# The attention of the first two batches on 64-row tiles, with a new order for every engine

## The chip, the cores and the metric

The kernel runs on one core of one Trainium2 chip. Times are device microseconds (us) of one execution of the whole program; the number that counts is the median of several runs. A profile comes from one further execution, in which each instruction's start and length was recorded. Names: PE is the matrix engine (PEld its weight loads), DVE the vector engine, ACT the scalar engine, POOL the GpSimd engine and SP the queue that issues most of the DMAs.

## The reference, cut to what matters

```python
kv  = einsum('bhsd,bhse->bhde', k, v)          # 8 batches, 8 heads, 576 rows, 64 columns
out = einsum('bhsd,bhde->bhse', q, kv)
x   = out / sqrt(mean(out**2) + 1e-6) * g_norm # per row and head
x   = x.transpose(0, 2, 1, 3).reshape(8, 576, 512)
u, v = split(relu(x @ w_in), 2)                # w_in is 512 x 1024
v   = (v - mean(v)) / sqrt(var(v) + 1e-6)
out = (u * (w_spatial @ v + b_spatial)) @ w_out
```

The attention has no softmax: per head it is two small products, a 64 x 64 matrix from 576 rows of keys and values, and 576 rows of queries times that matrix. The weights `w_in` and `w_out` arrive as 64-bit floats and are decoded on the chip.

## The kernel before

The eight heads of a batch are taken as four pairs. 512 of the 576 rows are the main part, four chunks of 128; the last 64 rows of two batches are put side by side and form a tail tile. The attention of a pair is a step K (keys times values, evicted from PSUM to SBUF as a small matrix), a step A or D (queries times that matrix, then squares and their sums), a step B (reciprocal root, and the scaling of the rows), and a step T (a transpose, whose eviction applies `g_norm` and writes x transposed). Then come the products with `w_in` (v half: H and `hv`, u half: u and `u_unit`), the layer norm, the spatial product (s, `sp_0`, `sp_steps`) and the output product (`out_unit`).

Batches 2 to 7 already do their attention on tiles of 64 rows and 64 columns, four of which lie in the array at once (`part_k`, `part_q`, `part_t`, `square`, `normal`, `turn_over`, `tail_norm`, `tail_turn`, scheduled by `later_steps`); they work on two pairs at a time. Batches 0 and 1 use functions of their own: `att_k` (from L202, products at L209) makes a 128 x 128 block-diagonal matrix of two heads, and `att_qa` (product at L284) multiplies queries of 128 rows by it; `norm_a` and `norm_b` square and scale 512 columns, `att_t` transposes four 128 x 128 blocks, and `att_end`, `tail_a`, `tail_b` and `att_tail` do the tail rows.

Batch 0 is special in its products with `w_in`: while the weights are being loaded and decoded, x is kept as one fp32 tile (X32) and H, u and h run in fp32 (L625, L663, L631). All later products use pairs of fp32r tiles, high and low part, in three products (L571, L538, L804). One H is `psv[c] += X32[pair k, chunk c] * W32[k]`, so H of pair k needs T of pair k and the k-th decoded weight.

The opening (batch 0, the attention of batch 1, and the loading, decoding and splitting of all weights) is written out by hand as a list of steps, `PLAN`. Its letters: L lets the next attention load go, W issues the next weight load (`w_in` in eight pieces of 512 KB, W0 to W7; then `w_spatial`, `b_spatial`, `w_out`), c and C decode a weight piece (one ACT instruction, then five of DVE, L954 to L958), H, u, h, s are the products above, e, F, f, y the ReLU, layer norm and splitting of v, X and E the splitting of weights into high and low part, Y sums of weights, Q and O decoding and splitting of a piece of `w_out`. At the end of the program the table `ORDER` gives, for each engine, the order of all its instructions, as positions in what is left of the program's own order; each engine runs strictly in that order.

In the opening PSUM has four banks for the products (`ps_mm`), three single banks for the attention and one for the tail; after it the last four banks become two slots of two banks each.

Of the kernel before, what the change touches and what calls it, by code (L numbers as in the profile page):

```python
# [33 lines left out]
PINNED = (mybir.EngineType.PE, mybir.EngineType.Activation, mybir.EngineType.SP)  # L34
PLAN = """

[ L W N8 G J00 L c C D00 W n6 L W J01 c B00 C L D01 J02 T00 B01 W D02 H00 c H30 H20 J03 T01 B02 D03
T02 H10 W c W H31 B03 L C L C H21 c H22 C H11 W W H32 a0 c W H01 T03 C c H02 H23 H03 H12 ] H33 e2
H13 e3 b0 L e1 C K10 F1 L L e0 W t0 c u00 C f2 F0 y2 L y0 F3 u01 D10 y1 W K12 u02 X3 a1 Z u03 L y3
u10 b1 X2 B10 t1 W W E1 L E0 A11 u11 W Q0 z u12 h D12 u13 W B12 T10 s s | s X1 T12 X0 s B11 D13 X5  # L40
B13 T11 X7 s s s s Y1 Y0 X4 P T13 O0 Q1 X6 W | p O1 R
# [21 lines left out]
""",  # L63
    "Activation": """
# [11 lines left out]
""",  # L76
    "DVE": """
# [21 lines left out]
""",  # L99
    "SP": """  # L100
# [3 lines left out]
""",  # L104
    "Pool": """
0.6 2.2 4.2 0.8 2 1 0.3 1 0 1 0 2 1 0.3 1 0.6 1 0 1 0
# [9 lines left out]
def body(ctx: ExitStack, tc, qT, qtl, kvm, kvt, g2, w_in, wsT, bsp, w_out, out):  # L116
# [9 lines left out]
    opening = ExitStack()  # L126
    ps_att = opening.enter_context(tc.tile_pool(name="ps_att", bufs=3, space=bass.MemoryType.PSUM))
    ps_tail = opening.enter_context(tc.tile_pool(name="ps_tail", bufs=1, space=bass.MemoryType.PSUM))
# [50 lines left out]
    def att_load(b, p, kind):  # L179
        if kind in "feko":  # L180
# [4 lines left out]
            r = p % 2 * TAIL if b > 1 else 0  # L185
            nc.sync.dma_start(kt[r:r + TAIL], kvt[b, p])
            keys[b, p] = kv, kt, None
# [4 lines left out]
        if kind == "k":  # L192
            qs = load.tile([P, P], F32, name="qs", tag="qs")
            nc.sync.dma_start(qs, qT[b, p, :, S - P:S])
            keys[b, p] = kv, kt, qs
# [6 lines left out]
    def att_k(b, pairs, st, copy=nc.vector.tensor_copy):  # L202
# [9 lines left out]
        for p in reversed(pairs):  # L212
            kv, kt, qs = keys.pop((b, p))
            for c in range(NC + 1):
                of = kv[:, :, c] if c < NC else kt
                for h in (0, D):
                    if first is None:
                        first = product(p, of, h, c).ins
                    else:
                        with tc.high_priority(), tc.issue_after(first):  # L220
                            product(p, of, h, c)
# [751 lines left out]
    def make_out(k):  # L973
# [3 lines left out]
        if pin:  # L977
            pin()
# [346 lines left out]
```

## Time and profile before

| what | us |
|---|---|
| median of 3 runs | 496.46 (495.97 to 496.64) |
| the profiled execution, its own time | 497.11 |
| its span, first to last instruction | 495.3 |
| PE busy, share of the span | 479.4 (97%) |
| DVE busy | 415.8 (84%) |
| ACT busy | 286.5 (58%) |
| POOL busy | 21.1 (4%) |

The span is what the trace covers; the 1.8 us between it and the execution's own time lie around it. An engine's busy time is the union of its instructions' lengths; instructions of one engine overlap by a little, so on an engine that never waits the cost of an instruction is the distance from its start to the next start, which is shorter than its length. The granted PE clock is 0.996 of full speed over the whole span.

### The profile page before, as it was taken

The numbers are of one execution on the slowest core, as the hardware profiler recorded it, in microseconds if no ns is written. First come the engines' busy times: TensorE is split into PE (matmuls) and PEld (weight loads), VectorE is DVE, ScalarE is ACT, GpSimd is POOL, SyncE is SP. The second block draws the span as 40 slices with busy tenths as digits, with TensorE's granted clock in tenths as the row PEclk, the third lists the DMA queues.
The fourth block names the chain that finished last, engine by engine and source line by source line (L and its number), as shares of the span: only waits on it lengthen the run. The fifth ranks groups of instructions, "written<-read, shape, count | busy, mean of one in ns | idle before, by whom it ended". The sixth has DMA issues, their size and how long they took to land.

```text
span 495.3 us, 11993 instructions
## 1 busy us (share of the span) xinstructions
PE 479.4 (97%) x4560; PEld 417.4 (84%) x4560; DVE 415.8 (84%) x1248; ACT 286.5 (58%) x913; POOL 21.1 (4%) x46
## 2 busy tenths in 40 slices
PE   6899999999999999999989999999999999999996
PEld 6658698798888899889977889988998899888985
DVE  1899889899899889988769789898888899998870
ACT  3757964697535855466423784547454587438331
POOL 5000000000000001000000001000000001000000
PEclk9999999999999999999989999999999999999999
DMA  7998100576524508135644514415571252215313
GB/s 240 356 337 271 42 3 21 154 249 242 181 71 149 194 7 297 50 98 174 227 156 149 171 44 151 159 65 161 163 273 56 44 192 89 84 44 170 108 73 98
DMA packets 28079, 71.99 MB, mean 145 GB/s; under 512 B 3506, under 2 KB 8626, under 8 KB 26484
## 3 DMA queue, kind: packets, MB, share of 16 engines
q1 hardware_dynamic: 24564, 49.19, 29.6%
q0 software_dynamic: 3456, 22.02, 13.4%
q8 instruction: 36, 0.59, 0.5%
q14 instruction: 23, 0.19, 0.1%
HBM read 58.09 MB, written 13.11 MB: 144 GB/s over the span
## 4 chain that ended last, share of the span: by engine, by line
PE 66%; DVE 13%; ACT 10%; DMA 8%; issue 2%; SPq 1%; POOL 0%; ACTq 0%; DVEq 0%
PE pso L538 18%; PE psh L571 10%; PE psb L804 6%; PE psa L804 6%; PE psub L804 4%; PE psc L804 4%; PE psh L625 3%; PE psuc L804 3%; DMA stage<-w_in 3%; PE psua L804 2%; DMA WO<-spare_o 2%; DMA qs<-qtl 2%; PE pskv L366 2%; DVE VL L575 2%; PE psu L663 1%
## 5 line engine op out<-in xcount | busy, mean ns | idle before, releaser
L538 PE MATMUL pso<-WO,G 128*128 128x512 f32 x384 | 98.3, 397 | 1.9 <-DMA WO<-spare_o 1.9
L538 PEld LDWEIGHTS pso<-WO,G 128*128 128x128 f32 x384 | 69.6, 189 | 16.8 <-DVE r L253 2.1
L574 ACT CAST G<-g 128x288 fp32r<-128x288 f32 (+1 forms) x56 | 22.8, 408 | 38.0 <-DVE g L823 37.8
L571 PE MATMUL psh<-WVH,XL 128*128 128x512 f32 x112 | 43.7, 390 | 0.0
L571 PE MATMUL psh<-WVL,XH 128*128 128x512 f32 x112 | 43.7, 390 | 0.0
L571 PE MATMUL psh<-WVH,XH 128*128 128x512 f32 x112 | 43.6, 395 | 0.0
L575 DVE TENSOR_TENSOR VL<-v,VH 128x512 fp32r<-128x512 f32 (+1 forms) x56 | 34.0, 621 | 6.1 <-ACT VH L574 6.0
L574 ACT CAST VH<-v 128x512 fp32r<-128x512 f32 (+1 forms) x56 | 31.0, 568 | 10.9 <-DVE v L603 9.1
L903 ACT COPY o<-pso 128x512 f32<-128x512 f32 x35 | 20.1, 587 | 22.1 <-PE pso L538 20.4
L558 ACT ACTIVATE v<-v,mv,rv 128x512 f32<-128x512 f32 x29 | 23.6, 814 | 8.6 <-DVE mv L557 7.2
L305 ACT ACTIVATE XH<-pstr,gcol 128x512 fp32r<-128x512 f32 x28 | 19.2, 696 | 15.9 <-PE pstr L473 7.1
L550 DVE BATCH_NORM_STATS2 s<-v 128x6 f32<-128x512 f32 x35 | 23.8, 688 | 3.4 <-ACT v L544 2.8
L804 PE MATMUL psb<-WSH,VH 128*128 128x288 f32 x84 | 26.2, 312 | 0.0
L544 ACT ACTIVATE v<-psh 128x512 f32<-128x512 f32 x32 | 19.1, 597 | 11.9 <-PE psh L571 10.8
L804 PE MATMUL psb<-WSH,VL 128*128 128x288 f32 x84 | 25.2, 300 | 0.0
L804 PE MATMUL psb<-WSL,VH 128*128 128x288 f32 x84 | 25.2, 300 | 0.0
L571 PEld LDWEIGHTS psh<-WVH,XH 128*128 128x128 f32 x112 | 20.9, 188 | 4.7 <-ACT WVH L962 0.2
L575 DVE TENSOR_TENSOR G<-g,G 128x288 fp32r<-128x288 f32 (+1 forms) x56 | 23.2, 419 | 2.0 <-ACT G L574 1.6
L571 PEld LDWEIGHTS psh<-WVH,XL 128*128 128x128 f32 x112 | 21.0, 188 | 4.4
L571 PEld LDWEIGHTS psh<-WVL,XH 128*128 128x128 f32 x112 | 21.0, 188 | 4.2 <-DVE WVL L963 0.2
L306 DVE SCALAR_TENSOR_TENSOR XL<-pstr,gcol,XH 128x512 fp32r<-128x512 f32 x28 | 20.8, 745 | 2.2 <-ACT XH L305 2.1
L1133 POOL DMA_DIRECT2D UX<-spare_u x12 | 6.5, 544 | 302.4 <-DVE T L575 150.4
(295 smaller groups left out, 1424.7 us busy)
## 6 DMA issues: line engine op xcount, KB each, us to landing
KV<-kvm SPq DMA_DIRECT2D x31, 512.0 KB, 5.5
WO<-spare_o POOLq DMA_DIRECT2D x12, 1024.0 KB, 6.3
UX<-spare_u POOLq DMA_DIRECT2D x12, 768.0 KB, 5.9
out<-o SPq DMA_DIRECT2D x32, 256.0 KB, 2.6
qt<-qT SPq DMA_DIRECT2D x28, 256.0 KB, 5.4
stage<-w_in SPq DMA_DIRECT2D x8, 512.0 KB, 6.5
KT<-kvt SPq DMA_DIRECT2D x32, 64.0 KB, 5.5
stage<-w_out SPq DMA_DIRECT2D x4, 512.0 KB, 4.5
```

The lines of the kernel that those rows point to most:

```text
L305: nc.scalar.activation(hi, ps, AF.Copy, scale=gcol)
L306: nc.vector.scalar_tensor_tensor(lo, ps, gcol, f32(hi), op0=ALU.mult, op1=ALU.subtract)
L538: nc.tensor.matmul(ps, lt, rh, start=i == 0, stop=i == n - 1)
L544: nc.scalar.activation(v, ps, AF.Relu)
L550: nc.vector.bn_stats(s6, v)
L558: nc.scalar.activation(v, v, AF.Identity, bias=m, scale=r)
L571: nc.tensor.matmul(ps, lt, rh, start=k == 0 and i == 0, stop=k == NP - 1 and i == 2)
L574: nc.scalar.copy(hi, x)
L575: nc.vector.tensor_tensor(lo, x, f32(hi), op=ALU.subtract)
L625: nc.tensor.matmul(psv[c], X32[:, k, c * P:(c + 1) * P], W32[k], start=k == 0, stop=k == NP - 1)
L804: nc.tensor.matmul(ps, lt, rh, start=start and i == 0, stop=stop and i == len(pairs) - 1, skip_group_check=True)
L903: nc.scalar.copy(o, ps)
```

## The change

Batches 0 and 1 use the 64-row functions too, and the old ones go. Batch 0 takes one pair at a time: K, A and T of a pair share one slot of two PSUM banks (columns 256 to 319 for K, 0 to 255 for A, 256 to 511 for T). Batch 1 takes two pairs at a time, as the later batches do. PSUM has two slots of two banks from the beginning. The tail rows go through `part_t`, `tail_norm` and `tail_turn`. With these functions the small matrix of K is evicted by an ACT copy and a DVE addition, not by two ACT copies.

```diff
     def part_k(b, pairs):
         banks, products = two_banks("pskv"), []
+        if b == 0:
+            states[b]["o", pairs] = banks
         def product(p, of, r, h, begin, end):
-            at, own = p % 2 * D, slice(r * TAIL, (r + 1) * TAIL)
+            at, own = p % 2 * D if b else NC * D, slice(r * TAIL, (r + 1) * TAIL)
...
-            nc.scalar.copy(to, banks[0][:, 0:2 * D])
-            nc.vector.tensor_tensor(to, banks[1][:, 0:2 * D], to, op=ALU.add)
+            nc.scalar.copy(to, banks[0][:, own])
+            nc.vector.tensor_tensor(to, banks[1][:, own], to, op=ALU.add)
...
     def square(b, pairs, st):
-        if pairs[0]:
+        if b == 0:
+            parts = [(work.tile([P, DM], F32, name="x", tag="x"), 0, NC)]
+        elif pairs[0] and b > 1:
             parts = [(stage2.tile([P, 2 * DM], F32, name="xx", tag="stage"), 0, 8)]
...
     def turn_over(b, pairs, st):
-        banks, x, products = two_banks("pstr"), st.pop(("x", pairs)), []
+        banks, x, products = st.pop(("o", pairs)), st.pop(("x", pairs)), []
+        if b:
+            banks = two_banks("pstr")
...
+                if b == 0:
+                    nc.scalar.activation(x32, ps, AF.Copy, scale=gcol)
+                else:
+                    split_x(ps, hi, lo)
...
-        "K": lambda b, p: att_k(b, (p, p + 1), st[b], nc.scalar.copy), "A": lambda b, p: att_qa(b, p, st[b]),
-        "B": lambda b, p: att_qb(b, p, st[b]), "T": lambda b, p: att_t(b, p, st[b]),
+        "K": lambda b, p: row(part_k(b, two(b, p))), "A": lambda b, p: row(part_q(b, two(b, p), st[b])),
+        "D": lambda b, p: square(b, two(b, p), st[b]), "B": lambda b, p: normal(b, two(b, p), st[b]),
+        "T": lambda b, p: turn_over(b, two(b, p), st[b]),
+        "a": lambda b: row(part_t(b, st[b])), "b": lambda b: tail_norm(b, st[b]),
+        "t": lambda b: tail_turn(b, st[b]),
```

`PLAN` and all five tables of `ORDER` are new, for the whole program; `pinned`, `in_turn`, `mark` and `keep_in_program_order`, which held parts of the old order, are gone. Read against the plan, position by position, the new tables begin as follows (K00 is K of batch 0, pair 0; KV, KT and q are the loads of keys and values, of their last 64 rows, and of queries; K10 and K12 stand for two pairs each, as do A10, A12, T10 and T12).

- SP: KV00, KT00, g, q00, W0, KV01, KT01, q01, W1, W2, W3, W6, KV02, KT02, a tail load, q02, a tail load, bias and last rows of `w_spatial`, W4, W5, KV03, KT03, q03, W7, a piece of `w_spatial`, KV10, and so on.
- PE: 14 products that only keep it busy, K00, A00, K01, A01, T00, four H of pair 0, K02, T01, A02, four H of pair 1, K03, A03, T02, two H of pair 2, a0, H, T03, H, four H of pair 3, t0, K10, ten u and more, K12, a1, u, t1, A10, h, A12, s, and T10 and T12 among the s.
- DVE after the decoding of W3 has begun: `K02 C3 C2 C3 C2 C3 D02 C4 D02 X1 C4 D02 C4 B02 C5 B02 C4 B02 K03 B02 C4 C6 X3 C6 D03` (one name for each instruction or two; C3 is one of the five instructions that decode W3). After it come the rest of C5 to C7, the two tails, the eight E, five more X, all of Q0, and then the layer norms F, the y, and h.

The old order issued KV02 and its queries ahead of W2, and W3 to W5 after the loads of pair 3. On DVE the old order had two of the eight X ahead of the first s and six behind it; in the new one seven of them stand ahead of the layer norms F.

## Rows read from the trace of the kernel before

**Rows 1.** Busy time of each engine in stretches of the span: from and to, length, then busy us and number of instructions of PE, PEld, DVE, ACT and POOL, the granted PE clock, the mean busy share of the DMA engines, and what they moved in GB/s.

```profile
10.00:15.00 5.00, 2.82 (x36) 2.30 (x35) 3.98 (x11) 4.15 (x27) 0.00 (x0) 1.00 1.04 375
15.00:20.00 5.00, 4.48 (x39) 3.25 (x40) 4.21 (x13) 4.36 (x33) 0.00 (x0) 1.00 1.05 324
20.00:25.00 5.00, 5.00 (x44) 3.35 (x43) 4.06 (x11) 3.52 (x21) 0.00 (x0) 1.00 1.01 385
25.00:30.00 5.00, 5.00 (x14) 2.25 (x13) 4.60 (x14) 2.84 (x7) 0.00 (x0) 1.00 1.05 359
30.00:45.00 15.00, 15.00 (x132) 10.57 (x131) 15.00 (x46) 9.00 (x34) 0.00 (x0) 1.00 0.96 325
45.00:60.00 15.00, 14.14 (x71) 11.28 (x70) 12.69 (x43) 14.75 (x36) 0.00 (x0) 1.00 0.23 73
100.00:130.00 30.00, 29.03 (x419) 25.77 (x412) 28.60 (x85) 22.19 (x75) 0.00 (x0) 1.00 0.67 221
130.00:495.00 365.00, 357.96 (x3438) 317.94 (x3429) 307.01 (x930) 198.54 (x599) 14.55 (x27) 0.99 0.39 130
```

**Rows 2.** PE in order of time in the opening: start, length, engine, line, operation, tiles, tile of the array, shape, how many instructions in a row (an fp32 product is two), and in brackets the idle time before and what ended it. L209 is K, L284 is A, L237 the tail's part of A, L312 is T, L625 is H, L663 is u, L804 is s, and L571 the first `hv` of batch 1.

```profile
11.51 0.69 PE L209 MATMUL pskv<-KV 128*64 128x64 f32 x16 [0.87 <-DMA KV<-kvm]
...
15.37 0.69 PE L209 MATMUL pskv<-KV 128*64 128x64 f32 x16 [0.92 <-DMA KV<-kvm]
...
16.91 1.16 PE L284 MATMUL pso<-KVB,qt 128*128 128x128 f32 x8
17.90 0.39 PE L237 MATMUL pst<-KVB,qt 128*128 128x128 f32 x2
18.12 2.74 PE L625 MATMUL psh<-RL,RH 128*128 128x512 f32 x6
20.79 0.69 PE L209 MATMUL pskv<-KV 128*64 128x64 f32 x16
21.31 0.29 PE L209 MATMUL pskv<-KT 128*64 128x64 f32 x4
21.53 0.65 PE L312 MATMUL pstr<-ident,x 128*128 128x128 f32 x4
...
23.34 0.60 PE L312 MATMUL pstr<-ident,x 128*128 128x128 f32 x4
23.77 6.17 PE L625 MATMUL psh<-RL,RH 128*128 128x512 f32 x14
...
31.18 0.68 PE L209 MATMUL pskv<-KV 128*64 128x64 f32 x16
...
32.49 4.56 PE L625 MATMUL psh<-RL,RH 128*128 128x512 f32 x10
36.89 0.65 PE L663 MATMUL psu<-RH,RL 128*128 128x288 f32 x2
...
63.28 0.38 PE L804 MATMUL psa<-WSH,hip 128*128 128x288 f32 x1
...
80.08 1.20 PE L571 MATMUL psh<-WVH,XH 128*128 128x512 f32 x4
```

**Rows 3.** PE in order of time in later batches, where the attention already runs on 64-row tiles; columns as in rows 2. L366 is K of two pairs (72 instructions), L395 A of two pairs, L473 T of two pairs (16 instructions), and L804 a product of the spatial step.

```profile
306.82 0.29 PE L804 MATMUL psb<-WSL,VH 128*128 128x288 f32 x1
307.04 0.74 PE L366 MATMUL pskv<-KV 64*64 64x64 f32 x34
...
308.14 1.11 PE L395 MATMUL pso<-KVO,qt 64*64 64x64 f32 x64
309.18 0.40 PE L804 MATMUL psc<-WSH,VH 128*128 128x288 f32 x1
...
316.83 0.71 PE L473 MATMUL pstr<-ident,x 64*128 64x64 f32 x16
317.38 0.66 PE L473 MATMUL pstr<-ident,xx 64*128 64x64 f32 x16
317.97 0.97 PE L538 MATMUL pso<-WO,G 128*128 128x512 f32 x3
```

**Rows 4.** DVE, first three instructions in order of time in the opening (start and length), then groups of instructions by line and shape: how many, busy us and mean ns of one, and the idle time before them. L276 and L449 scale the rows after A (old and new functions), L441 sums squares, L383 is the addition that evicts K.

```profile
33.06 0.68 DVE L955 SCALAR_TENSOR_TENSOR stage<-stage,t 128x512 uint32<-128x512 uint32 x1
33.67 0.42 DVE L954 TENSOR_SCALAR t<-t 128x512 uint32<-128x512 uint32 x1
34.00 0.16 DVE L255 SCALAR_TENSOR_TENSOR rh<-qh,rh 128x8 f32<-128x8 f32 x1
...
L276 DVE TENSOR_TENSOR x<-pso,rh 128x512 f32<-128x512 f32 x8 | 5.4, 687 | 0.3
...
L449 DVE TENSOR_TENSOR x<-pso,r 128x256 f32<-128x256 f32 x24 | 9.2, 417 | 0.1
...
L441 DVE TENSOR_REDUCE s<-x 128x4 f32<-128x256 f32 x12 | 4.9, 413 | 0.1
...
L383 DVE TENSOR_TENSOR KVO<-pskv,KVO 128x128 f32<-128x128 f32 x6 | 1.7, 288 | 2.1 <-ACT KVO L382 2.1
```

**Rows 5.** ACT in order of time when the first weight piece has landed; columns as in rows 2.

```profile
9.93 0.66 ACT L948 ACTIVATE t<-stage 128x512 f32<-128x512 f32 x1 [3.29 <-DMA stage<-w_in]
```

**Rows 6.** The two waits of PE over 0.8 us between the first 20 us and 100 us: the fp32 tail product h, and the first K of batch 2; columns as in rows 2.

```profile
59.38 3.70 PE L631 MATMUL psh<-RL,RH 128*128 128x512 f32 x8 [0.86 <-ACT RH L326]
...
90.23 0.74 PE L366 MATMUL pskv<-KV 64*64 64x64 f32 x34 [1.10 <-DVE XL L306]
```

More of the change, by code (lines that the diff above doesn't have):

```diff
@@ L33 @@
 NB = B
-PINNED = (mybir.EngineType.PE, mybir.EngineType.Activation, mybir.EngineType.SP)
 PLAN = """
[L37 to L41, printed above, removed]
+L L W N8 G K00 L L c C A00 D00 W n6 W K01 c B00 C A01 D01 T00 L L W K02 c B01 H00 H30 H20 A02 D02 T01 C H10 L L K03
+W c W H31 B02 A03 D03 T02 H21 L C H22 H11 W W H32 a0 c B03 H01 b0 T03 C c H02 H23 H03 t0 H12 H33 e2 H13 e3 L L e1 C
+K10 F1 L L e0 W c u00 f2 F0 y2 L W y0 F3 C u01 y1 W K12 c a1 C u02 X3 b1 Z u03 t1 L L y3 u10 A10 X2 D10 W W E1 L L E0
+u11 W Q0 z u12 h B10 A12 u13 W s T10 D12 s s X1 X0 s B12 X5 T12 X7 s s s s Y1 Y0 X4 P O0 Q1 X6 W p O1 R
 """
@@ L184, in att_load @@
                 nc.sync.dma_start(kv[:, :, i:j], kvm[b, p, :, :, i:j])
-            r = p % 2 * TAIL if b > 1 else 0
+            r = p % 2 * TAIL
             nc.sync.dma_start(kt[r:r + TAIL], kvt[b, p])
-            keys[b, p] = kv, kt, None
+            keys[b, p] = kv, kt
         if kind == "s":
@@ L191, in att_load @@
                 nc.sync.dma_start(tails[b, j], qtl[b, j])
[L192 to L195, printed above, removed]
-        if kind in "fq":
-            n = NT if b % 2 or b > 1 else S
-            qt = load.tile([P, S], F32, name="qt", tag="qt")
-            nc.sync.dma_start(qt[:, 0:n], qT[b, p, :, 0:n])
-            queries[b, p] = qt
-    def att_k(b, pairs, st, copy=nc.vector.tensor_copy):
-        ps = ps_att.tile([P, 512], F32, name="pskv", tag="att")
-        to = KVO[pairs[0] // 2] if b % 2 else KVB
-        ends, first = [], None
-        def product(p, of, h, c):
-            at = (p - pairs[0]) * P + h
-            return nc.tensor.matmul(ps[h:h + D, at:at + D], of[:, 0, h:h + D], of[:, 1, h:h + D],
-                                    start=c == 0, stop=c == NC)
[L212 to L221, printed above, removed]
-            st[p] = to[:, p % 2]
-            ends.append((p, qs))
-        both = ps[:, 0:len(pairs) * P].rearrange("p (j e) -> p j e", e=P)
-        own = slice(p % 2, p % 2 + len(pairs))
-        copy(to[0:D, own, 0:D], both[0:D, :, 0:D])
-        nc.scalar.copy(to[D:P, own, D:P], both[D:P, :, D:P])
-        for p, qs in reversed(ends):
-            if qs is not None:
-                att_end(p, st, qs)
-        issue()
-    def att_end(p, st, q):
-        if p == 0:
-            st["tail"] = ps_tail.tile([P, 512], F32, name="pst", tag="tail")
-        nc.tensor.matmul(st["tail"][:, p * P:(p + 1) * P], q, st[p], start=True, stop=True)
+        if kind == "q":
+            queries[b, p] = qt = load.tile([P, NT], F32, name="qt", tag="qt")
+            nc.sync.dma_start(qt, qT[b, p, :, 0:NT])
     def rsqrt(ss, n, rows, mul, tag):
@@ L369, in part_k @@
         for p in reversed(pairs):
-            kv, kt, _ = keys.pop((b, p))
+            kv, kt = keys.pop((b, p))
             for c in range(NC + 1):
@@ L388, in part_q @@
     def part_q(b, pairs, st):
-        banks, products = two_banks("pso"), []
-        st["o", pairs] = banks
+        if b:
+            st["o", pairs] = two_banks("pso")
+        banks, products = st["o", pairs], []
         def product(i, qt, c, h, r):
@@ L432, in square @@
             parts = [(work.tile([P, DM], F32, name="x", tag="x"), i * NC, NC) for i in range(2)]
-        ss = small.tile([P, 16], F32, name="s2", tag="s2")
+        m = sum(n for _, _, n in parts)
+        ss = small.tile([P, 16], F32, name="s2", tag="s2")[:, 0:2 * m]
         ps = st["o", pairs]
@@ L440, in square @@
             nc.scalar.activation(turned(x, n, 1), heads(ps[1][:, at * D:(at + n) * D]), AF.Square)
[L441 to L442 removed]
+            nc.vector.tensor_reduce(ss[:, m + at:m + at + n], turned(x, n, 1), axis=AX.X, op=ALU.add)
+        st["n", pairs] = parts, m, rsqrt_a(ss, 2 * m, P, 1.0 / D, "2")
     def scale(ps, parts, m, small_parts):
@@ L467, in turn_over @@
     def turn_over(b, pairs, st):
-        banks, x, products = two_banks("pstr"), st.pop(("x", pairs)), []
+        banks, x, products = st.pop(("o", pairs)), st.pop(("x", pairs)), []
+        if b:
+            banks = two_banks("pstr")
+        own = slice(0, DM) if b else slice(NC * TAIL, 2 * NC * TAIL)
         def product(i, c, r):
-            rows, at = slice(r * TAIL, (r + 1) * TAIL), (i * NC + c) * TAIL
+            rows, at = slice(r * TAIL, (r + 1) * TAIL), own.start + (i * NC + c) * TAIL
             return nc.tensor.transpose(banks[r][:, at:at + TAIL], x[i][rows, c * P:(c + 1) * P], ident[rows, rows])
@@ L476, in after @@
             for r, ps in enumerate(banks):
-                hi, lo = (x[:, pairs[0]:pairs[0] + 2, r * (NT // 2):(r + 1) * (NT // 2)] for x in (XH, XL))
-                split_x(ps.rearrange("p (i t) -> p i t", i=2), hi, lo)
-        row(([lambda a=(i, c, r): product(*a) for i in range(2) for c in range(NC) for r in range(2)], after))
+                x32, hi, lo = (x[:, pairs[0]:pairs[-1] + 1, r * (NT // 2):(r + 1) * (NT // 2)]
+                               for x in (X32, XH, XL))
+                ps = ps[:, own].rearrange("p (i t) -> p i t", i=len(pairs))
+                if b == 0:
+                    nc.scalar.activation(x32, ps, AF.Copy, scale=gcol)
+                else:
+                    split_x(ps, hi, lo)
+        row(([lambda a=(i, c, r): product(*a) for i in range(len(pairs)) for c in range(NC) for r in range(2)],
+             after))
     def tail_turn(b, st):
@@ L1051, in ahead @@
         issue()
[L1053 removed]
+    nc.vector.memset(KVO[1][:, 1], 0.0)
     nc.vector.memset(epsc, EPS)
     nc.scalar.activation(small.tile([P, 1], F32, name="warm", tag="av"), epsc, AF.Sqrt)
[L1056 to L1060 removed]
     make_identity(nc, ident)
     def warm(n):
[L1065 removed]
+        ps = two_banks("psw")[0]
         for _ in range(n):
[L1067 to L1085 removed]
+            nc.tensor.matmul(ps[:, 0:P], KVO[1][:, 1], KVO[1][:, 1], start=True, stop=True)
     def filler(n):
         for _ in range(n):
[L1089 to L1090 removed]
+            nc.tensor.matmul(psv[3][:, 0:P], KVO[1][:, 1], KVO[1][:, 1], start=True, stop=True)
     queue = []
@@ L1095, in enqueue @@
         if b < NB:
-            queue.extend(att_steps(b)[late])
+            queue.extend(later_steps(b)[late])
     def step(n=1):
@@ L1139, in to_out @@
             nc.gpsimd.dma_start(WO[:, i], spare_o[:, i])
-    turn = {}
-    def mark(name, f):
-        def g(*a):
-            f(*a)
-            if name not in turn or a[0] == 1:
-                turn[name] = next(i for i in reversed(nc.cur_bb.bb.instructions)
-                                  if i.engine == mybir.EngineType.Activation)
-        return g
-    def in_turn(f):
-        def g(*a):
-            with tc.issue_after(turn["a"]):
-                f(*a)
-        return g
     loads = [lambda k=k: load_in(1, k) for k in range(NP)]
@@ L1167, in body @@
     st = [states.setdefault(b, {}) for b in range(2)]
+    two = lambda b, p: (p, p + 1) if b else (p,)
     do = {
@@ L1181, in body @@
         "s": lambda: sp_0(*units.pop(0)), "X": split_in, "E": split_ws, "z": split_tail,
-        "Z": blank_tails, "P": outw, "p": gates, "Q": in_turn(make_out), "O": split_out, "R": split_g,
+        "Z": blank_tails, "P": outw, "p": gates, "Q": make_out, "O": split_out, "R": split_g,
     }
-    hold = behind = None
     for token in PLAN.split():
-        if token in "[]":
-            hold = pinned() if token == "[" else hold()
-        elif token == "|":
-            behind = next(i for i in reversed(nc.cur_bb.bb.instructions)
-                          if i.engine == mybir.EngineType.DVE)
-        else:
-            with tc.issue_after(behind) if behind else ExitStack():
-                do[token[0]](*map(int, token[1:]))
-    opening.close()
-    ps_att = ctx.enter_context(tc.tile_pool(name="ps_att", bufs=2, space=bass.MemoryType.PSUM))
+        do[token[0]](*map(int, token[1:]))
     ahead(len(todo))
```

163 lines of the change are left out of this document (28 added, 135 removed), and 107 rows, old and new, of the table ORDER.

## The prediction

> **What bounds the kernel now.** I read the busy times by stretch first [rows 1]. From 20 us on PE is the bound: busy for 5.00 of 5 us, and 357.96 of 365 us after 130 us. So whatever leaves PE's queue there is time gained, as long as nothing else becomes late. Ahead of 20 us the loads are the bound: the DMA engines are full (1.04, 1.05) while PE is busy for 2.82 and 4.48 of 5 us. The second thing to see is DVE: between 30 and 45 us it is busy for 15.00 of 15 us, as PE is; it decodes the weights there and has no room. The third is PE in order of time [rows 2]: K waits for its keys at 11.51 and 15.37, the first H starts at 18.12, the first u at 36.89, the first s at 63.28, the first `hv` at 80.08. I use these four starts as milestones. Two waits of PE follow in this part, 0.86 and 1.10 us [rows 6].
>
> **What leaves PE.** In the old form a pair costs: K 0.74 (20.79 to 21.53), 0.10 for going from H into it (three H take 2.57 of the 2.67 us from 18.12), A 0.99 (16.91 to 17.90), its tail part 0.22, T 0.43 (23.34 to 23.77) [rows 2]; 2.48 in all. Two K together take 1.31 (31.18 to 32.49), 0.66 each. With two tail transposes of a T's size, 0.43 each, batch 0 costs 4 x 2.48 + 0.43 = 10.4 and batch 1 about 9.7: 20.1 us. In the new form [rows 3] K of two pairs takes 1.10 (307.04 to 308.14), A of two 1.04 (308.14 to 309.18), T of two 0.55 to 0.59 (316.83, 317.38, 317.97). Going in costs 0.09 (0.22 from 306.82 to 307.04, where neighbouring products of this size are 0.13 to 0.16 apart); the way out, some 0.13, is in the last instruction of a block. The Trainium skill (TensorEngine Tiling (Array Packing), Key Properties) says that changing the tiling mode drains the engine; these rows show that price at about 0.2 us for an excursion, and if it were free the sum below would be some 3 us better. One pair, half of two without the way out: K 0.48, A 0.46, T 0.25, and 0.37 for the switches, 1.56; four of them with the tail (bounded by half of A, 0.2 to 0.5, and 0.22 for the two transposes) 6.9. Batch 1: 2 x 1.19 + 2 x 1.13 + 2 x 0.7 for K, A, T and about 0.9 for the tail, 7.0. Together 13.9 us in place of 20.1: **6.2 us less on PE.**
>
> **What DVE and ACT get.** On an engine that never waits an instruction costs the distance between starts: 0.61 for 512 columns (33.06 to 33.67), 0.33 for the next (33.67 to 34.00), so 0.085 less than its own length [rows 4]. Then DVE has, for each pair of batch 0, a new addition (0.20, from 288 ns for 128 columns; here 64), a new sum of squares (0.33, from 413 ns), and two scalings of 256 columns (0.33 each, 417 ns) in place of one of 512 (0.60, 687 ns): +0.59, +2.4 for four. The tails have half the columns: -0.47 each. Batch 1 gets 2 additions, 4 sums and 8 scalings in place of 4 scalings and a sum of 512, and saves two sets of five small instructions of 0.09: +0.5. Sum **+1.9 us on DVE**. ACT loses work (half as many squares are taken one by one, at two instructions each); it is not the bound before 45 us (9.00 of 15 us) [rows 1].
>
> **The opening, step by step.** Nothing about the first pair moves much: W0 lands at 9.93 [rows 5], KV01 at 11.51 [rows 2]. DVE then decodes W0 (five instructions, 0.33 + 0.60 + 0.33 + 0.60 + 0.60 = 2.47) and between them scales the rows of pair 0; that ends near 14.2, T00 follows at once since it is no longer behind a K that waits for keys, its first eviction ends near 15.8. **First H at 15.8, not 18.12: 2.3 us won.**
>
> Then the new load order takes back. W2, W3 and W6 (512 KB each) now go ahead of KV02: 1.5 MB more, at 324 GB/s [rows 1] 4.6 us, so KV02 lands at 20.0 instead of 15.37. The four H of pair 0 last till 19.5 (0.86 each): PE waits 0.5. Next KV03: 2.2 MB behind KV02 at 385 to 359 GB/s, 5.8 us, 25.8. PE has T01, A02 and four H till 26.2, so K03 finds its keys. But K03's new addition stands in DVE's fixed order behind a queue: from the end of pair 1's scaling (21.2 by the same addition of costs) one instruction of W3, then K02's addition (22.0), then 0.33 + 3 x 0.60 + 0.60 for C3 and C2, and for D02, C4, X1, C5 and B02 another 4.0, with small ones between: K03's addition ends at **28.9**. PE has finished K03 at 26.8 and waits 2.1 us, then once more 0.8 for the eviction of T02. With the same 0.86 per H the first u starts at 39.8, **2.9 us later than before**. (This stretch has 4.3 us of waits that the old one had not; PE's 2.7 us of saving for pairs 1 to 3 are in it.)
>
> From u to s the old stretch is 26.4 us (36.89 to 63.28). Out of it go K (1.41), two tail products and two tail transposes (1.8), three A (2.9), T (0.36 of it ahead of s) and the wait of 0.86 to 1.0: 7.4. In come K12 1.19, a1 0.66, t1 0.22, A10 and A12 2.27: 4.3. So 23.3 us, **first s at 63.1**, level with before. DVE's own chain to that point, added up in the new order from 28.9 (C4 to C7, the norms of pair 3 and the tails, 8 E, five more X at 0.60, all of Q0, four F, y), ends at about 62.7 if it never idles: just in time.
>
> From s to the first `hv`, 16.8 us before: out go T, A, T (1.9), in come two T of two pairs (1.46): 16.4, so 79.5, **0.6 us won**. Behind it go the last T of batch 1 (0.4) and most of the wait of 1.10 us for the slot of the first K of batch 2, since that slot's last owner is now evicted earlier: 2.0 to 2.2 us in all. Later batches do the same work in another order; PE's room there is small (7 us of 365), and I count it as 0, +-1.5.
>
> The profiled execution took 497.1 (span 495.3 and 1.8 around it); less 2.2 this is 494.9, and it lies 0.65 above the median of 496.46. **Forecast: 494.2**, its own range 492.3 to 496.0.
>
> **Rivals.**
> - *All of PE's saving lands.* If DVE's queue runs ahead of my sum (28.9 for K03's addition is the sum of some thirty costs), the 2.1 and 0.8 us vanish, and the rest follows: 496.46 - 6.2 = 490.3. For it: DVE starts dense at 10 us, where it now has 0.8 to 1.0 us idle in each 5 [rows 1]. Against it: no spare room up to 45 us.
> - *The loads come later still.* If KV03 lands at 28 instead of 25.8, everything from K03's addition on moves with it, 1 to 1: +2.2, so 496.4, no change. The point is where the landing and PE's 0.6 for K pass DVE's 28.9. For it: 324 GB/s for the whole way instead of 385.
> - *DVE becomes the bound, and it is slower.* DVE has 33 us of work between K03's addition and the last y, and s cannot start without the y; seven X and Q0, which nothing needs before `hv` or the output product, stand ahead of the layer norms (five X after K03, 3.0 us, and Q0 2.5). Up to now it hides, with a margin of 0.4 us. From 45 to 60 us DVE idles 2.3 of 15 us [rows 1] because it hands data back and forth with ACT. If it idles as much over these 33 us, it ends 5.1 us later, s starts at 67.8, and with the later gains of 0.4 + 0.4 + 1.0 the end is 496.46 + 4.5 - 1.8 = 499.2; with half of that idling about 496.7. From some 2.3 us of idling on it is slower than before. The Trainium skill (TensorEngine Tiling (Array Packing), PSUM Bottleneck) says that tiling speeds up the matrix engine and not the emptying of PSUM, which may become the bound; that is this rival, and the +1.9 us on DVE agree with it.
>
> **How the numbers follow.** Forecast 0.45, all saved 0.22, later loads 0.14, DVE slower 0.19. A difference of 0.2% is 1.0 us, about what a measurement of this kernel can tell from no change. Faster: 0.41 of the forecast's 0.45 and 0.22, 0.63. Same: 0.04, 0.11 of the loads, 0.02 of DVE, 0.17. Slower: 0.20. The range goes down to 490.0, just past all saved, and up to 498.0, halfway into the slower case.
>
> **What would show it.** First H near 15.8; a wait of PE near 20 for keys and one of about 2 us near 27 with K03's addition on DVE late; first u near 39.8, first s near 63, first `hv` near 79.5; DVE with no idle time between 11 and 60. PE's blocks of K, A, T in batches 0 and 1 should add up to about 14 us. First u at or before 37 would mean the first rival; a wait ahead of s of more than 2 us, with DVE or ACT as releaser, the last.

## The result, and the profile after

The changed kernel takes 501.47 us (median of 20 runs, 497.93 to 504.35), the kernel before 496.71 in the same series: ratio 1.0085, 95% interval 1.0066 to 1.0103, slower by 4.2 us by the ratio, clear of the noise. Forecast were 494.2, with a range up to 498.0. The profiled execution is one of the shortest: 498.29, span 496.5, mean granted clock 0.986; the runs at the median have 0.977 to 0.980, the longest ones 0.974 to 0.976.

Stretches of the span, changed kernel (columns as in [rows 1]):

```profile
12.25:19.10 6.85, 5.31 (x44) 2.94 (x45) 6.27 (x18) 3.78 (x16) 0.00 (x0) 0.50 1.00 357
19.10:29.30 10.20, 8.20 (x126) 4.27 (x125) 9.68 (x28) 8.34 (x24) 0.00 (x0) 1.00 0.89 307
29.30:36.20 6.90, 6.33 (x61) 3.37 (x62) 5.30 (x15) 4.31 (x17) 0.00 (x0) 0.51 0.96 327
36.20:45.00 8.80, 8.80 (x101) 4.98 (x102) 7.21 (x22) 8.03 (x22) 0.00 (x0) 1.00 0.54 151
```

The clock column is what [rows 1] did not have: all the stretches there up to 130 us stand at 1.00. Now TensorE had half its clock (1.2 of 2.4 GHz) in two stretches of the opening. PE in order of time (columns as in [rows 2]; L256 is K, L286 A, L370 T, L508 H, L546 u):

```profile
10.76 0.69 PE L256 MATMUL pskv<-KV 64*64 64x64 f32 x32 [2.24 <-DMA KV<-kvm]
...
12.25 1.13 PE L286 MATMUL pskv<-KVB,qt 64*64 64x64 f32 x32 [0.69 <-DVE KVB L273]
...
15.62 5.41 PE L508 MATMUL psh<-RL,RH 128*128 128x512 f32 x8 [1.24 <-ACT RH L378]
...
22.95 3.70 PE L508 MATMUL psh<-RL,RH 128*128 128x512 f32 x8
27.44 0.69 PE L256 MATMUL pskv<-KV 64*64 64x64 f32 x32 [0.79 <-DMA KV<-kvm]
...
29.29 1.13 PE L286 MATMUL pskv<-KVB,qt 64*64 64x64 f32 x32 [1.04 <-DVE KVB L273]
...
31.61 3.78 PE L508 MATMUL psh<-RL,RH 128*128 128x512 f32 x4 [0.56 <-ACT RH L378]
...
43.41 2.94 PE L546 MATMUL psu<-RH,RL 128*128 128x288 f32 x11
```

Four H (x8) last 3.70 at the full clock and 5.41 when the half clock covers a part of them; two H (x4) last 3.78, where [rows 2] has three in 2.74. The engine had waited 2.24 and 0.69 us ahead of the first stretch, 0.79 and 1.04 ahead of the second. First H is at 15.62 (forecast 15.8), first u at 43.41 (39.8), first s at 67.04 (63.1).

The largest waits of PE in the whole run (waiting line and what it waited for: us in total, times, longest; three more follow, of 1.1 us and less):

```profile
PE pskv L256 <- DMA KV<-kvm: 3.0, 2, 2.2
PE pskv L286 <- DVE KVB L273: 2.5, 4, 1.0
PE pso L286 <- issue: 2.1, 1, 2.1
PE psh L508 <- ACT RH L378: 1.8, 2, 1.2
...
```

The two waits of [rows 6] are gone. The third line is new, and lies at 359 us, in attention that the change does not touch. "issue" says that the profile names nothing that PE waited for. PE there, in order of time:

```profile
356.74 0.74 PE L256 MATMUL pskv<-KV 64*64 64x64 f32 x34
...
357.83 1.03 PE L286 MATMUL pso<-KVB,qt 64*64 64x64 f32 x57
360.98 0.34 PE L286 MATMUL pso<-KVB,qt 64*64 64x64 f32 x7 [2.11 <-issue]
```

PE stops behind product 57 of the 64 of one A. The DMA queues tell what was missing. First 356.7 to 358.6 us, then 358.6 to 359.8 (packets, bytes, share of the 16 DMA engines; q0 carries the reload of the output weights, WO):

```profile
DMA packets 98, 0.76 MB, mean 401 GB/s; under 512 B 5, under 2 KB 5, under 8 KB 5
...
q0 software_dynamic: 98, 0.76, 101.1%
```

```profile
q0 software_dynamic: 68, 0.47, 100.2%
q8 instruction: 1, 0.02, 5.2%
```

q8 is a queue that brings instructions, in packets of 16 KB; 38 of them come in this run, for 9848 recorded products and weight loads of PE, some 259 for each (36 for 9120 before, some 253). In the first stretch the reload fills the DMA engines and no packet of q8 moves; it moves in the second, from 358.7 to 359.7, while PE runs dry at 358.9. PE goes on at 360.98, 1.3 us behind the packet's end. The rest of the profile agrees with [rows 4, 5]: the scaling of 256 columns takes 418 ns, the first weight piece reaches ACT at 9.65.

### The profile page after: what moved, and what is told of

It reads as the page before. It is cut to its first block, busy times and chain, and to the rows that moved or that the text cites. A ratio compares the mean times of both kernels' runs of the same rounds, so it can differ in the third digit from the quotient of the medians.

```text
span 496.5 us, 12673 instructions
## 1 busy us (share of the span) xinstructions
PE 480.3 (97%) x4924; PEld 412.7 (83%) x4924; DVE 417.7 (84%) x1261; ACT 282.7 (57%) x870; POOL 19.5 (4%) x41
## 4 chain that ended last, share of the span: by engine, by line
PE 82%; DVE 7%; ACT 5%; DMA 3%; issue 1%; POOL 0%; ACTq 0%; DVEq 0%
PE pso L421 19%; PE psh L454 13%; PE psb L687 6%; PE psa L687 6%; PE psc L687 4%; PE psub L687 4%; PE psu L546 3%; PE pskv L256 3%; PE psua L687 3%; PE psh L508 3%; PE psu L421 3%; PE psuc L687 3%; DMA WO<-spare_o 2%; PE pso L286 2%; PE pstr L370 1%
## 5 line engine op out<-in xcount | busy, mean ns | idle before, releaser
L421 PE MATMUL pso<-WO,G 128*128 128x512 f32 x384 | 95.3, 395 | 0.1
L421 PEld LDWEIGHTS pso<-WO,G 128*128 128x128 f32 x384 | 69.8, 188 | 15.8 <-DVE G L458 0.7
L457 ACT CAST VH<-v 128x512 fp32r<-128x512 f32 (+1 forms) x56 | 30.8, 565 | 10.1 <-DVE v L486 9.3
L441 ACT ACTIVATE v<-v,mv,rv 128x512 f32<-128x512 f32 x29 | 23.4, 817 | 10.6 <-DVE mv L440 10.0
L256 PEld LDWEIGHTS pskv<-KV 64*64 64x64 f32 x1024 | 18.2, 134 | 7.6 <-issue 7.1
```

The lines of the kernel that those rows point to most:

```text
L256: return nc.tensor.matmul(banks[r][h:h + D, at:at + D], of[own, 0, h:h + D], of[own, 1, h:h + D], start=begin, stop=end)
L421: nc.tensor.matmul(ps, lt, rh, start=i == 0, stop=i == n - 1)
L441: nc.scalar.activation(v, v, AF.Identity, bias=m, scale=r)
L457: nc.scalar.copy(hi, x)
```

## The experiments

Ratios are to the kernel before, beside it on the same chip, with 95% intervals; its median was 496.1 to 497.0 in the four series. Theory A was that the half clock of the opening makes the loss, theory B that the later loads and VectorE's queue do and the clock is only beside it. The first runs overthrew both as the main cause.

**The changed kernel again** (`c0_changed_again`), no edit.

> The changed kernel itself once more, as the yardstick on the same chip. Both theories: ratio 1.006 to 1.011 to the kernel before. Theory A (the loss is two stretches of the opening in which the granted TensorE clock is 0.5, about 12 to 19 us and 29 to 36 us): the profile shows both again, at 11 to 20 us and 28 to 38 us, and the runs that are longer than the first profiled one (498.3 us at a mean clock of 0.986) have a lower mean clock, so a third or fourth stretch at 0.5 somewhere. Theory B (the waits for the later loads and the VectorE queue cost it, the clock is only beside it): the stretches may come and go, and the first u product stands at 43 us either way.

500.59 us, ratio 1.008 (1.005 to 1.011). Its profiled execution took 502.87; both opening stretches are there, first u at 44.54, and a third one behind the wait in A, which is 3.3 us here:

```profile
PE pso L286 <- issue: 3.3, 1, 3.3
```

```profile
357.00:361.90 4.90, 2.84 (x135) 2.60 (x135) 3.13 (x10) 1.12 (x4) 0.00 (x0) 1.00 1.04 381
361.90:368.80 6.90, 5.70 (x41) 5.46 (x41) 2.56 (x5) 4.09 (x21) 0.00 (x0) 0.51 0.77 265
```

From the start of the first u to that of the last product PE needs 448.7 us in the first profile (43.4 to 492.1) and 452.1 here (44.5 to 496.6).

**Fillers in TensorE's waits** (`e1_fill`, `e2_fill_first`, `e3_fill_second`): products that nobody reads, put into the order behind the named step. `e1` has both lines, `e2` the first, `e3` the second. The code here and below is shortened to what matters.

```diff
+    def busy(n, to, behind):
+        for _ in range(n):
+            extra.append((behind, nc.tensor.matmul(to, KVO[1][:, 1], KVO[1][:, 1], start=True, stop=True).ins))
+    EARLY = {'A00': 9, 'K01': 2, 'A01': 1, 'T00': 5}
+    LATE = {'H11': 4, 'K03': 4}      # ahead of K03, and behind it
```

> The changed kernel with 25 more fp32 128x128 products that nobody reads, in the idle places of TensorE: 17 ahead of the first H (9 behind the first A, 2 behind the second K, 1 behind the second A, 5 behind the first T), 4 ahead of the fourth K and 4 behind it. No real instruction is moved, and each filler takes 0.22 us at the full clock. Theory A: granted clock 1.00 from 0 to 60 us, first H at 15.6 to 16.0, first u product at 39.3 to 40.0 instead of 43.4, first s at 62.8 to 63.6 instead of 67.0, and the time falls by 3 to 4 us: ratio to the kernel before 0.997 to 1.003. Theory B: the fillers can only be in the way: first u at 43 or later, ratio 1.008 to 1.012.

> The changed kernel with the 17 fillers ahead of the first H alone. Theory A: the stretch at half clock around 12 to 19 us goes and the one around 29 to 36 us stays (the wait for the fourth pair's k and its addition is as long as before); the first four H products take 3.5 us instead of 5.4, the first u comes about 1.7 us earlier (41.7), the ratio is 1.7 us lower than the changed kernel's: about 1.005. It may be less, if the second wait then grows because the fourth pair's k lands when it lands. Theory B: no change of the ratio, 1.008 to 1.011.

> The changed kernel with the 8 fillers around the fourth K alone. Theory A: the first stretch at half clock stays, the second goes; first u about 2.2 us earlier than in the changed kernel (41.2), ratio about 1.004. Theory B: no change of the ratio, 1.008 to 1.011.

All three win more, some 5 us, than the earlier first u can explain: 0.9987 (0.9965 to 1.0010), 0.9983 (0.9963 to 1.0003) and 0.9958 (0.9939 to 0.9978), 495.71, 495.41 and 494.59 us. The clock did what theory A said: 1.00 up to 60 us in `e1`, one stretch left in `e2` (30.8 to 34.2) and `e3` (12.0 to 18.9). But first u is at 41.59, 42.18 and 41.64, only 1.2 to 1.8 earlier, and `e1` reaches it no earlier than `e3`: without the first stretch the first four H take 3.85 instead of 5.28, and K03 still starts at 27.76, when its keys are there. Where the second place has its fillers, the first stretch costs nothing. (In `e2`, which has none there, the second stretch is 3.4 us long instead of 6.9, so the two are not independent. The profile of `e1` also has a wait of 1.91 us for ACT at 400.85, with a half clock stretch behind it, that `e3` has not.) The rest of the gain goes with the wait at 359 us, which all three have lost. That I had not expected, and it made the second question.

**The same number of instructions without the work** (`e5_tiny`).

```diff
-    nc.tensor.matmul(to, KVO[1][:, 1], KVO[1][:, 1], ...)
+    nc.tensor.matmul(to[0:1, 0:1], KVO[1][:, 1, 0:1], KVO[1][:, 1, 0:1], ...)
```

> As the run with fillers at the second place only (4 ahead of the fourth K, 4 behind it), but each filler is 1x1 instead of 128x128: as many instructions on TensorE at the same places, next to no work. It parts two causes. Clock: the second stretch at 0.5 (29 to 36 us) comes back, first u at 42.8 to 43.6. Instructions: in the changed kernel TensorE waited 2.1 and 3.3 us near 359 us in an A while a 16 KB transfer of its instruction queue was under way, and with 8 or more fillers 0.0 to 0.2. If that wait hangs on where the blocks of 16 KB end among the instructions, it stays away here (under 0.5 us), and the ratio is 1.001 to 1.004, between 0.996 and 1.008. If it came from the slower opening (the loads, or the clock), it is back at 2 to 3 us and the ratio is 1.006 to 1.010.

495.8 us, ratio 0.9989 (0.9965 to 1.0013). The half clock is back in both places and first u as late as in the changed kernel, 44.05:

```profile
12.90:19.80 6.90, 5.38 (x41) 2.68 (x32) 6.61 (x18) 4.42 (x16) 0.00 (x0) 0.51 0.96 322
30.00:36.90 6.90, 6.33 (x62) 3.38 (x62) 4.96 (x14) 4.06 (x18) 0.00 (x0) 0.51 0.86 287
```

And the A runs through:

```profile
357.65 1.11 PE L288 MATMUL pso<-KVB,qt 64*64 64x64 f32 x64
```

So 32 instructions of no work, 300 us earlier, bring the ratio from 1.008 to 0.999 (0.009, about 4.5 us), and keeping the clock up as well, in `e3`, another 0.003 (about 1.5 us; the two intervals overlap, but first u shows 2.4).

**256 instructions** (`e6_shift256`): `e3`, and 56 products of 1x1 behind A00.

```diff
-    EARLY = {}
+    EARLY = {'A00': 56}              # 1x1
```

> As the run with 128x128 fillers at the second place, and 56 products of 1x1 more behind the first A, in TensorE's idle 2.5 us there: with the 8 fillers that makes 64 products more than in the changed kernel, 256 instructions (each fp32 product is two, each with its weight load), which is one transfer of 16 KB by the count of the trace (some 253 recorded instructions for each). Instructions theory: all later blocks end again where they end in the changed kernel, so the wait of 2 to 3.3 us in an A near 356 us is back although the opening is fast; ratio 1.000 to 1.006. Rival (the wait comes from the slow opening): no such wait, ratio 0.994 to 0.998. The 56 small products should take under 2.5 us and delay nothing that counts.

502.17 us, ratio 1.0126 (1.0104 to 1.0149). The wait is back, 2.82 us, behind product 58 of the same A, though the second place keeps its fillers:

```profile
361.38 1.09 PE L288 MATMUL pso<-KVB,qt 64*64 64x64 f32 x58
365.29 0.34 PE L288 MATMUL pso<-KVB,qt 64*64 64x64 f32 x6 [2.82 <-issue]
```

The 56 were not free, though I had expected them to be: PE ran dry in the opening too, 2.7 us inside K01 (again "issue"), and first u came at 46.44, 4.8 us later than in `e3`. That is enough to take it beyond the range named.

**8 and 16 instructions** (`e12_tiny2`, `e13_tiny4`): the changed kernel with 2 and 4 products of 1x1 behind K03.

```diff
-    LATE = {}
+    LATE = {'K03': 2}                # 4 in the other; 1x1
```

> The changed kernel with 2 products of 1x1 between the fourth K and its A, in TensorE's wait there: 8 instructions more, nothing else. If TensorE ran dry because the next 16 KB of instructions are asked for when the block ahead of them is entered, and that happens at the start of the K of two pairs at 356.7 us, then 8 instructions move this entry 4 products (0.13 us each) ahead of K: the wait in A is some 0.5 us shorter than the 2.1 to 3.3 us of the changed kernel, 1.5 to 2.8, and TensorE stops about 4 products earlier in A (53 instead of 57 of 64). Ratio 1.003 to 1.009. Rival (any shift frees it): no wait, ratio 0.997 to 1.001.

> The same with 4 products of 1x1, 16 instructions: the entry lies 8 products, some 1.1 us, ahead of K; the wait is 1.0 to 2.2 us, or less if the transfer of the instructions is then asked for ahead of the reload of the output weights; TensorE stops at 49 of 64. Ratio 1.000 to 1.007. Rival (any shift frees it): no wait, ratio 0.997 to 1.001.

501.14 us, ratio 1.0079 (1.0049 to 1.0110), and 497.39, ratio 1.0014 (0.9988 to 1.0040). A in the one and in the other:

```profile
358.84 0.99 PE L288 MATMUL pso<-KVB,qt 64*64 64x64 f32 x54
362.30 0.44 PE L288 MATMUL pso<-KVB,qt 64*64 64x64 f32 x10 [2.47 <-issue]
```

```profile
360.34 0.98 PE L288 MATMUL pso<-KVB,qt 64*64 64x64 f32 x50
362.45 0.45 PE L288 MATMUL pso<-KVB,qt 64*64 64x64 f32 x14 [1.13 <-issue]
```

PE stops behind product 57, 54, 50 (a product of A is one weight load and one product, so 8 instructions are 4 of them; 53 and 49 were expected). The waits, each read from one profile, are 2.1 and 3.3 without, 2.5 with 8, 1.1 with 16, none with 32.

**Without the reload** (`e11_no_reload`): the output weights are not loaded again but set to zero, so this kernel leaves out part of the work.

```diff
-            nc.gpsimd.dma_start(WO[:, i], spare_o[:, i])
+            nc.gpsimd.memset(f32(WO[:, i]), 0.0)
```

> The changed kernel, in which the reloads of the output weights (two DMAs of 1 MB for each batch) are left out and GpSimd writes zeros there instead. Near 356 us that reload fills the DMA engines. If it is the traffic that makes the 16 KB of instructions late, the wait in A near 359 us shrinks from 2.1 and 3.3 us to 0.0 to 0.7, and the transfer of the instruction queue starts within 1 us of K's start (356.7) instead of 2 us behind it; the time falls by 2 to 5 us, ratio 0.998 to 1.004. If 256 small instructions in 2.1 us are too fast for that queue in any case, the wait stays at 2 us or more and the ratio at 1.005 to 1.010. VectorE may be slowed by GpSimd's writing.

The wait in A is gone, and the packet of instructions moves at 357.6 to 358.7, as K starts (357.99), with the queues otherwise empty:

```profile
359.09 1.29 PE L286 MATMUL pso<-KVB,qt 64*64 64x64 f32 x64
```

```profile
DMA packets 1, 0.02 MB, mean 15 GB/s; under 512 B 0, under 2 KB 0, under 8 KB 0
...
q8 instruction: 1, 0.02, 5.0%
```

The time did not follow: 499.53, ratio 1.0064 (1.0033 to 1.0094). Its profile has another wait, 2.3 us for VectorE at 418 us with 3.4 us at half clock behind it, and first u at 44.79. It shows what the wait hangs on, not what it costs.

The reload is not all of it. In `e1` (100 instructions more than the changed kernel) PE stops in another A, at 229 us, where the DMA engines are nearly idle: the packet moves from 227.03, as K starts at 227.01, and still comes 0.2 us too late. In `e9` below (84 more) the same A has a wait of 0.58. Two lines of PE in order of time in `e1`, and the stretch ahead of them:

```profile
228.11 0.99 PE L288 MATMUL pso<-KVB,qt 64*64 64x64 f32 x55
229.31 0.38 PE L288 MATMUL pso<-KVB,qt 64*64 64x64 f32 x9 [0.21 <-issue]
```

```profile
225.00:229.30 4.30, 4.10 (x143) 3.74 (x141) 3.85 (x9) 2.50 (x7) 0.00 (x0) 1.00 0.10 26
```

So K and A of two pairs are just too dense for a packet that starts with K; the reload makes it start later (1.95 us behind K's start in the first profile, 2.9 in the second) and the wait about as much longer.

**The kernel before, 36 instructions fewer** (`e8_before_wide`).

```diff
-        for _ in range(n):
-            nc.tensor.matmul(ps[:, 0:P], KVB[:, 1], KVB[:, 1], start=True, stop=True)
+        for _ in range(n // 4):      # 512 columns; the later fillers n // 2, 256 columns
+            nc.tensor.matmul(ps, KVB[:, 1], wide, start=True, stop=True)
```

> The kernel before with its 14 opening fillers (128 columns each) as 5 wider ones (two of 512 and three of 256 columns): the same columns in the same places, 9 fp32 products and so 36 instructions fewer. By the count of the trace the kernel before enters a block of 256 instructions 36 ahead of the K of two pairs at 359 us, in which a reload of the output weights fills the DMA engines; in the changed kernel that entry lies within 2 of the start of the same K, and TensorE ran dry 256 instructions further on, in A. Instructions theory: now the kernel before waits too, 2 to 3.5 us in an A or T near 361 us with the profile naming no releaser, ratio 1.003 to 1.009, though nothing of its attention has changed. Rival (the wait belongs to the changed order or the slow opening): no such wait, ratio 0.998 to 1.002.

A wait appears where it should, behind product 51 of the A of the same pairs, but of 0.67 us, and the time does not rise: 495.05, ratio 0.9975 (0.9952 to 0.9999).

```profile
359.81 0.45 PE L395 MATMUL pso<-KVB,qt 64*64 64x64 f32 x13 [0.67 <-issue]
```

Its packet of instructions moved between 356.7 and 358.3, by K's start at 357.07, and not 2 us behind it. In all ten waits of this kind in the profiles PE goes on 1.3 to 1.6 us behind the end of the packet. So the place of the block alone does not give the size of the wait; how long the packet is held up by the reload differs, and why, stays open.

**The fillers' place** (`e4_before_early_fill`: the kernel before with its six fillers ahead of the first K; `e10_fillers_back`: the changed kernel with them behind the first A).

```diff
-[ L W N8 G J00 L c C D00 W n6 L W J01
+[ L W N8 G n6 J00 L c C D00 W L W J01
```

```diff
-0.8 34.6 0.76 18 19 43
+0.90 18 19 43
```

> The kernel before with one thing of the change alone: its six fp32 fillers stand ahead of the first K, as in the changed kernel, instead of behind the first A and its tail (9.1 to 10.6 us). Theory A (TensorE idle in the wait for the second pair's keys brings the granted clock down): a stretch at 0.5 appears at 10 to 20 us, the first H products take up to twice as long, the first u comes 1 to 3 us later than 36.9, ratio 1.002 to 1.006. Theory B (the clock is only beside it): first H at 18.1 and first u at 36.9 as before, ratio 0.998 to 1.002. If K and its keys lie so that the later work waits anyway, the clock falls and the ratio still stays near 1.000: the starts of H and u then tell.

> The changed kernel with one part of the change undone: its six fillers go back from ahead of the first K to behind the first A, in the wait for the second pair's keys. The number of instructions ahead of all later blocks is that of the changed kernel. Clock theory of the opening: the first stretch at 0.5 (12 to 19 us) goes or gets shorter, the second stays, first u at 42 to 43.5. Instructions theory: the wait in A near 358 us stays at 2 to 3.3 us, and the ratio stays at 1.005 to 1.010. If the fillers' place were the cause of the loss, the ratio would fall to 1.001 or less.

`e4`: ratio 1.0021 (1.0000 to 1.0042), 497.53 us; half clock from 13.6 to 17.1, first H at 19.18, first u at 37.94, 1.05 later than before. `e10`: ratio 1.0048 (1.0021 to 1.0074), 498.55 us; the wait in A stays at 2.3, and the clock falls all the same (11.7 to 21.9, longer than before, and 32.2 to 35.6), first u at 43.72. The ratio is lower than the changed kernel's, but the intervals overlap; the fillers' place is at most a part of the loss, and the first stretch does not hang on it alone.

**Earlier keys** (`e7_keys`: `e3`, and KV03, KT03, q03 ahead of the tail weights, W4 and W5, K03's addition one decoding step earlier, its copy on ACT ahead of two casts; `e9_best`: `e1`'s early fillers, these keys, 4 fillers behind K03, none ahead).

```diff
-0.3 2 0.7 3 10 0.2 6 0 5 23.2 22 3.2 0.4 8
+0.3 2 0.7 3 10 0.2 6 0 5 0.3 20.2 19 0.3 8
```

> As the run with 128x128 fillers at the second place, and the fourth pair's k, v and q loaded ahead of the bias and tail weights and of W4 and W5, with its K addition on VectorE one decoding step earlier, and its copy on ScalarE ahead of two casts. It tests the step of the prediction on which K03 hangs. If the landing of the keys and the addition's place in VectorE's order hold the opening (27.4 and 29.0 us), K03 starts behind the H ahead of it without a wait (26.4), the addition is at 27.8 to 28.2, first u 0.7 to 1.2 us earlier than 41.6, ratio 0.992 to 0.996. If VectorE's whole queue holds it, the first u stays at 41.6 and the ratio at 0.996; if W4 and W5 come too late instead, H waits for them and it is slower than 0.996.

> The changed kernel with all three repairs: the 17 fillers ahead of the first H, the fourth pair's k, v and q loaded earlier with its addition one decoding step earlier, and 4 fillers between the fourth K and its A, none ahead of K. 21 products, 84 instructions, more than the changed kernel, so the block of instructions ends away from A. Clock theory: granted clock 1.00 up to 60 us, K03 at 25.8 to 26.4, first u at 40.0 to 41.0 instead of 41.6 (fillers at the second place alone), ratio 0.992 to 0.996. If it is VectorE's whole queue that holds the opening, first u at 41.6 and ratio 0.996 to 0.999.

0.9973 (0.9960 to 0.9987), 494.88 us, first u at 42.05; and 1.0003 (0.9974 to 1.0033), 496.38, first u at 45.12. No gain, and in `e9` neither of the two starts of u that were named: K03 is done by 26.7, but VectorE's queue stands still ahead of its addition, because ACT waits until 26.35 for a weight piece that lands later. VectorE in order of time:

```profile
27.05 0.43 DVE L804 TENSOR_SCALAR t<-t 128x512 uint32<-128x512 uint32 x1 [2.45 <-ACT t L798]
...
29.62 0.22 DVE L240 TENSOR_TENSOR KVB<-pskv,KVB 128x64 f32<-128x64 f32 x1
```

As far as these two runs show, it makes no difference whether keys or weights come first; the loads in total set the end of this stretch. `e9`'s own runs fall into two groups: six with a mean clock of 0.996 or more took 494.0 to 495.7, six with 0.993 or less 497.1 to 499.9. The profiled one (498.09, 0.992) has the second stretch; that the others of its group have it too is likely and not shown.

## Why the prediction was wrong

It failed in two steps; both took the same instructions to cost the same wherever they stand.

*"Later batches do the same work in another order ... and I count it as 0, +-1.5."* This step failed most. The work is the same, but it stands elsewhere in PE's stream of instructions. The change adds instructions to the opening (9120 recorded products and weight loads of PE in the whole run before, 9848 after), so the blocks of 16 KB end at other places in all later batches, and one of them ends inside an A while the reload of WO fills the DMA engines. K and A of two pairs are 272 instructions in 2.1 us, and [rows 3] shows the same density; a packet takes about 1 us, and PE goes on 1.3 to 1.6 us behind its end. Shown: the wait follows the shift (0, 8, 16, 32, 256 instructions), and nearly goes without the reload (none in `e11`, 0.2 and 0.6 where the DMA engines are nearly idle in `e1` and `e9`). It costs 2.1 to 3.3 us, and in one of the two profiles a stretch at half clock behind it; the lower mean clocks of the longer runs make that likely for many of them. From the ratios of the changed kernel and `e5` together it is about 4.5 us. Argued only: that a block is asked for when PE enters the one before it. It fits the count: K is 144 instructions, 57 products of A are 114, and K's start is thus 258 ahead of the stop; and with the DMA engines nearly idle (`e1`, `e9`, `e11`) the packet moves within 0.3 us of K's start.

*"With the same 0.86 per H the first u starts at 39.8."* All durations of the opening were taken at the full clock, since [rows 1] showed no other. The waits that this very step predicted around K03 (2.1 and 0.8; measured 0.79, 1.04 and 0.56) stand ahead of the second stretch and in its beginning, and products put there keep the clock up (`e3`, against `e5`). The wait of 0.5 at 20 us did not come; the first stretch stands behind waits of 2.24 and 0.69 at 10.8 and 12.3. So the waits between first H and first u were no longer than forecast, 2.6 us in all; the step names 3.4 (0.5, 2.1 and 0.8) and says 4.3. The first u was late all the same, since H ran in part at half clock: 5.41 for four and 3.78 for two, where 0.86 each was counted. With the clock kept up behind K03 (`e3`) the first u is at 41.6; an estimate without the 1.1 us of the four fillers in A03's way is 40.5, 0.7 off the forecast. In the changed kernel it is 43.4 to 44.5. The Trainium skill (TensorE: Matmul & The Clock Gate, HAM oscillation) describes such a trap, a wait for data that lets the clock fall so that the next products start slow; the two stretches above, behind waits of 0.8 to 2.2 us, are of that kind. The price by the ratios of `e5` and `e3` is about 1.5 us (their intervals overlap), by the first u 2.4.

The other steps:
- *First H at 15.8*: 15.62.
- *PE's blocks, 13.9 us*: one pair's K, A, T took 0.73 (20.95 to 21.68), 0.63 (22.32 to 22.95) and 0.40 (37.09 to 37.49), 1.76 instead of 1.56, some 0.8 for four; K of two pairs of batch 1 took 1.21 (42.20 to 43.41), forecast 1.19. By these the saving is there, some 5.4 instead of 6.2.
- *KV02 at 20.0, KV03 at 25.8, K03's addition at 28.9*: K02 found its keys by 19.5 (`e1`); KV03 landed at 27.4, nearly the second rival's 28; the addition starts at 29.02. That rival's premise was half right, but the addition was not held by the keys alone (`e7`, `e9`).
- *u to s 23.3*: 23.63 (43.41 to 67.04). *First hv 79.5*: 79.70, but the new order starts it ahead of two s units and a T, so it is no milestone and hid 3.7 us of loss.
- *Behind u, 5.1 us less than before*: without the wait in A (`e3`, `e5`) 445.3 and 445.5 instead of 453.9 us, 8.5 less; with it 448.7 and 452.1. So "0, +-1.5" missed a gain too, of some 3.4 us.
- *DVE becomes the bound*: no wait ahead of s, and none of PE's waits behind 44 us over 0.7 us but the one in A. The slower time came by none of the rivals.

Part of that gain can be seen in the profile before. It has a wait of 1.88 us for the reload of WO, with half clock behind it. The kernel before has this wait in `e4` and `e8` too (2.60 and 2.09 us), and no profile of the changed kernel has it; why the new order is free of it stays open. PE in order of time, and the stretch behind it, in the kernel before:

```profile
250.80 0.93 PE L538 MATMUL pso<-WO,G 128*128 128x512 f32 x3 [1.88 <-DMA WO<-spare_o]
```

```profile
252.00:255.80 3.80, 3.80 (x16) 3.53 (x16) 2.23 (x8) 0.95 (x3) 0.00 (x0) 0.55 0.07 19
```

So with the wait in A gone the edit comes out where it was forecast, and partly by luck: `e3`, the change with 8 idle products in two waits, takes 0.9958 of the time before, 2.1 us less (1.5 by the medians), and beats both kernels; the forecast was 2.2 less. But its first u is 1.8 later than forecast, and what is behind it some 3.5 shorter. What was missed is that the supply of instructions is a resource too.

## What to carry to other kernels

A change that adds or removes instructions on TensorE moves the ends of its instruction blocks in all the code behind it; before a difference far from the change is explained by its order, shift the stream by some idle instructions and measure again. When a new order puts waits between TensorE's blocks, as here 0.79, 1.04 and 0.56 us in a row, cost the products behind them at half clock too, or fill the waits. And a stretch that is bound by its loads gave nothing back here for putting one load ahead of another. When a forecast is met, check its terms too: here a late opening and a gain that nobody had counted made up for each other.

## What the runs showed of the hardware

- TensorE can wait for its own instructions: 2.1 to 3.3 us, and 2.7 us behind 112 products and 112 loads of 1x1 in 2.9 us (`e6`). The Trainium skill (Runtime: NRT & Kernel Launch, Instruction fetch mechanics) says that the next page is fetched while the current one runs and that the cost of crossing a boundary of 16 KiB is mostly hidden. The changed kernel agrees for all its blocks but one, which is the one wait of this kind in the list of PE; where dense 64-row blocks met full DMA engines, it was not hidden, and with the DMA engines nearly idle it still showed as 0.2 and 0.6 us (`e1`, `e9`).
- PE does not go on when the packet of instructions has moved, but 1.3 to 1.6 us later, in all ten such waits.
- A half clock stretch can be free: with the second place filled, the first one made four H 1.4 us longer (5.28 in `e3`, 3.85 in `e1`) and moved nothing behind it (first u at 41.64 and 41.59), because K03 waits for its keys, till 27.4 to 27.8, in any case.
- The clock is not the same in every run of one kernel: the wait in A had no half clock behind it in the first profile of the changed kernel, and had one in the second, with mean clocks of 0.986 and 0.976 and 498.29 and 502.87 us.
